# The order of split products inside each group: attention and the first MLP part

## The chip, the cores and the metric

One core of a Trainium2 chip. The metric is the device time of one execution in microseconds (us); lower is better. The engines are TensorE (PE, with its weight loads shown apart as PEld), VectorE (DVE), ScalarE (ACT), GpSimd (POOL) and SyncE (SP, which issues DMAs). Each takes its instructions in a fixed order and waits on semaphores for what others make.

## The reference

Linear attention with a feature map, then two MLP blocks, over 8 batches, 8 heads, 576 tokens, head width 64, model width 512. What matters here:

```python
def phi(x):
    proj = np.einsum('bhsd,df->bhsf', x, w_phi)
    proj = proj - np.max(np.abs(proj), axis=-1, keepdims=True)
    return np.concatenate([np.exp(proj), np.exp(-proj)], axis=-1)
q_p, k_p = (phi(q), phi(k))
kv = np.einsum('bhsf,bhsd->bhfd', k_p, v)      # key-value products, with z = sum of k_p beside them
num = np.einsum('bhsf,bhfd->bhsd', q_p, kv)    # numerators, with the denominators beside them
...
xn = (x - mu) / np.sqrt(var + 1e-06) * g_ln    # first MLP block
ch = np.maximum(xn @ w_ch1, 0.0) @ w_ch2
x = x + ch
...                                            # second block: cos and sin of x @ w_theta, token mixing, a channel MLP
```

All inputs are float32, and the kernel reaches that accuracy with the faster 32-bit matmul type by splitting: a value is the sum of a high part, rounded to that type, and a low part, the rest. A product of two split values is three matmuls into one PSUM accumulator: high by high, high by low, low by high.

## The kernel before, in words

**Attention.** 16 units (`Unit`), one for each of 4 pairs of batches and 4 pairs of heads, each with 9 token tiles of 128 in five groups (`GROUPS`: two tiles, two, one, two, two). The single tile of group 2 holds the last 64 tokens of one batch and the first 64 of the next, so it gives two slots of half zeros; in all there are ten slots. `keys` (line 310) makes the features of a group: `phi` (projection into PSUM tile `pj`, maximum `m`, difference `ys` on VectorE), two exponentials on ScalarE, the high part `kph` on ScalarE, then the low part `kpl` on VectorE (line 64; on GpSimd for two groups of the first five units). `values` (line 325) multiplies them with the split values `vh`, `vl` into the accumulator `kv`: for each slot and each of the two heads one call of `mm3`, that is three matmuls of 256 columns. The values are the stationary operand, and the features move. The key features are the factor made last.

`queries` makes the features of the queries, transposed, split into `qp` (high part by ScalarE, low part by GpSimd), and `numer` (line 404) multiplies them with the transposed key-value sums `kvh`, `kvl`: four accumulators `nm` in groups 2 and 4, each of two `mm3` calls of 288 columns. Units 0 to 4 do the numerators unsplit, unit 0 also the key-value products, each in one float32 matmul; these are not touched.

**First MLP part.** `Mlp` holds the first 4 of 16 hidden blocks of 128 (`NFA`), applied in attention's shadow to 18 chunks of 256 tokens. `mlp_a` normalises and transposes a chunk, splits it into `xh` (ScalarE) and `xl` (VectorE); `up` (line 189) makes two hidden blocks into a PSUM tile `ph`, each over 4 blocks of the model width, one `mm3` of 256 columns for each; `relu` splits the result into `hh` (ScalarE) and `hl` (VectorE); `down` (line 196) sums over the 4 hidden blocks into `ph` again, one `mm3` of 512 columns for each. After 650 us the rest of the kernel runs (the other 12 hidden blocks with fewer products by a matrix identity, then the second MLP block); the diff touches none of it.

**What sets the order.** The program is written as generators that are interleaved by `attention` and the loop behind it, but the order on each engine comes from a planner: it runs a model of all engines, and at each point gives an engine the instruction of highest rank (place in the program, moved by `high_priority`; the first MLP part is put back by 600 places, `MPRI`) whose inputs are there by that model. So matmuls of several accumulators come mixed on TensorE, but the matmuls of one accumulator stay in the program's order. On the chip each engine then follows the planned order, and an instruction that waits holds back all that is behind it. Accumulators are PSUM tiles: two for `pj`, one for `tr`, one for `kv`, two for `nm`, two for `ph`.

In the profile, `mm3` is lines 74 (high by high), 75 (stationary high by moving low) and 76 (stationary low by moving high). A trace row names the moving operand first: `kv<-kpl,vh` reads the low part of the key features.

Of the kernel before, what the change touches and what calls it, by code (L numbers as in the profile page):

```python
# [9 lines left out]
F32 = mybir.dt.float32  # L10
# [11 lines left out]
B, H, S, D = 8, 8, 576, 64  # L22
DM = 512
DFF = 2048
NF = 128
# [4 lines left out]
KC = DM // P  # L30
# [22 lines left out]
def body(ctx, tc, qT, kT, va, wbd, g, w1, w2, wth, wtok, wch, out):  # L53
    nc = tc.nc
    V, A, G, T, SY = nc.vector, nc.scalar, nc.gpsimd, nc.tensor, nc.sync
# [17 lines left out]
    def mm3(out_, lh, ll, rh, rl, start, stop, **kw):  # L73
        T.matmul(out_, lhsT=lh, rhs=rh, start=start, stop=False, **kw)  # L74
        T.matmul(out_, lhsT=lh, rhs=rl, start=False, stop=False, **kw)  # L75
        return T.matmul(out_, lhsT=ll, rhs=rh, start=False, stop=stop, **kw).ins  # L76
# [88 lines left out]
    class Mlp:  # L165
# [23 lines left out]
        def up(self, f, ph, xh, xl):  # L189
            h, l = self.w1[f // 2]  # L190
            for j in range(2):
                fs = slice((2 * (f % 2) + j) * P, (2 * (f % 2) + j + 1) * P)
                for c in range(KC):
                    mm3(ph[:, j, :], h[:, c, fs], l[:, c, fs], xh[:, c, :], xl[:, c, :], c == 0, c == KC - 1)

        def down(self, i, acc, hid):
            o = slice(i * P, (i + 1) * P)
            for f, (hh, hl) in enumerate(hid):
                for j in range(2):
                    wh, wl = self.w2[2 * f + j]  # L200
                    mm3(acc, hh[:, j, o], hl[:, j, o], wh, wl, f == 0 and j == 0, f == self.nf // 2 - 1 and j == 1)

        def relu(self, pool, ph):
            hh = pool.tile([P, 2, NC_], F32R, name="hh", bufs=2)
# [13 lines left out]
    ps_pj, ps_tr, ps_kv, ps_nm, ps_ph = pool("pj", 2), pool("tr", 1), pool("kv", 1), pool("nm", 2), pool("ph", 2)  # L218
# [26 lines left out]
    GROUPS = [[0, 1], [2, 3], [4], [5, 6], [7, 8]]  # L245
# [4 lines left out]
    class Unit:  # L250
# [74 lines left out]
        def values(self, gi, kh, kl):  # L325
            if gi == 0:
                self.acc = ps_kv.tile([D + 1, 2, 2 * NF], F32, name="kv")
            for i, t in enumerate(GROUPS[gi]):
                for sl in [t] if t < 4 else ([4, 5] if t == 4 else [t + 1]):
                    if sl == 5:  # L330
                        self.kv_done()
                        self.acc = ps_kv.tile([D + 1, 2, 2 * NF], F32, name="kv")
                    vh, vl = self.v[sl // 5]
                    for h in range(2):
                        j = 2 * i + h
                        rh = kh[:, j].rearrange("p s f -> p (s f)")
                        if kl is None:
                            T.matmul(self.acc[:, h, :], lhsT=vh[:, sl % 5, h, :], rhs=rh,
                                     start=sl in (0, 5) and h == 0, stop=sl in (4, 9), skip_group_check=True)
                            continue  # L340
                        rl = kl[:, j].rearrange("p s f -> p (s f)")
                        mm3(self.acc[:, h, :], vh[:, sl % 5, h, :], vl[:, sl % 5, h, :], rh, rl,
                            sl in (0, 5) and h == 0, sl in (4, 9), skip_group_check=True)
            if gi == 4:
                self.kv_done()

# [57 lines left out]
        def numer(self, gi):  # L404
            if gi in (2, 4):
                b = 0 if gi == 2 else 1
                kh, kl = self.kv[b]
                for h in range(2):
                    for hf in range(2):
                        nm = ps_nm.tile([D + 1, 288], F32, name="nm")  # L410
                        cs = slice(hf * 288, (hf + 1) * 288)
                        for s in range(2):
                            if kl is None:
                                T.matmul(nm, lhsT=kh[:, 2 * h + s, :], rhs=self.qp[b][0][:, h, s, cs], start=s == 0,
                                         stop=s == 1)
                                continue
                            mm3(nm, kh[:, 2 * h + s, :], kl[:, 2 * h + s, :], self.qp[b][0][:, h, s, cs],
                                self.qp[b][1][:, h, s, cs], s == 0, s == 1)
                        o = b * S + hf * 288
                        A.activation(self.num[:, h, o:o + 288], nm, AF.Copy)  # L420
                for t0 in [0] if b == 0 else [3, 6]:
                    self.norm(t0)
# [280 lines left out]
    def in_slot(n, slot, shape, dtype=F32R):  # L703
        return slot_pool(slot).tile([P, *shape], dtype, name="xs", tag=f"{n}{slot}")
# [15 lines left out]
    total, done, n = sum(w for _, w in work), 0, 0  # L720
    left = 6 * (NCH - 1 - chunk)
    for _ in gm:
        n += 1
        with tc.issue_after(ma.low), tc.issue_after(ma.high), tc.high_priority(offset=LOWP):
            while work and done < total * n / (left * SPREAD):
                g, w = work.pop(0)
# [466 lines left out]
    for r in range(2):  # L1193
        done = 0
        for ch in range(NQ):
            last = ch == NQ - 1
            if r and ch == LATE:
                t = in_slot("wa", 2, [7, DM])
                wths = [t[:, 2 * i:2 * i + 2] for i in range(3)]
                spare = f32(t[:, 6])  # L1200
                t = in_slot("wd", 2, [2, 2, DM])
                wths += [t[:, i] for i in range(2)]
            xs = cur
            acc = [ps_ac.tile([P, DM], F32, name=f"acc{i}") for i in range(2 * CT)]
# [50 lines left out]
    t = p_xb.tile([P, 4, 2, 2 * P], F32R, name="xs", tag="xt")  # L1255
# [198 lines left out]
```

## Time and profile before

| | |
|---|---|
| Time, median of 3 runs | 1651.89 us (1651.49 to 1654.31) |
| The profiled execution's own time | 1651.22 us |
| Its span, first to last instruction | 1649.4 us |
| TensorE busy (matmuls) | 1611.8 us, 98% |
| Weight loads busy | 1482.6 us, 90% |
| VectorE busy | 1270.1 us, 77% |
| ScalarE busy | 877.8 us, 53% |
| GpSimd busy | 715.4 us, 43% |
| Mean granted TensorE clock | 0.997 |

The shares are means over stages that differ. GpSimd, for one, does most of its work before 500 us. Matmuls are pipelined: the profile shows each with its full length, and the next starts before it ends, so the distance from start to start tells the rate. The number in brackets at the end of a row of the timeline is the time for which the engine stood idle before that instruction, and whose work ended it.

### The profile page before, as it was taken

To read this page: it belongs to the slowest core of one execution; us is meant where nothing else is said; L and a number is where in the kernel's file an instruction comes from. 1 tells how busy PE (TensorE), PEld (TensorE's weight loads), DVE (VectorE), ACT (ScalarE), POOL (GpSimd) and SP (SyncE) were. 2 spreads that over 40 slices of the span, in tenths; PEclk is the share of its full clock that TensorE was granted. 3 is DMA by queue.
4 is the path that set the end of the run, shared out by engine and by line. 5 is a ranking of instruction groups with operands and counts; after the bars stand their busy time and mean duration, and the time that the engine had idled before them with its cause. 6 is when DMAs were issued, how large, how long until landed. Compare 5 with 4: busy or idle time off the path is not lost.

```text
span 1649.4 us, 29031 instructions
## 1 busy us (share of the span) xinstructions
PE 1611.8 (98%) x11080; PEld 1482.6 (90%) x11080; DVE 1270.1 (77%) x2274; ACT 877.8 (53%) x1718; POOL 715.4 (43%) x561
## 2 busy tenths in 40 slices
PE   8899999999999999999999999999999999999998
PEld 6788999999999888899998989999889999999998
DVE  7989878888987774788777676778567878788784
ACT  6777767677776553445544434444444444544441
POOL 7876989899991001221111222211232443344430
PEclk9999999999999999999999999999999999999999
DMA  5334333333332644445547444463258565765754
GB/s 188 102 101 127 108 89 111 111 103 117 98 98 95 231 139 154 154 175 203 178 167 296 157 148 154 155 216 128 84 190 309 190 229 209 272 233 203 243 195 180
DMA packets 120329, 273.81 MB, mean 166 GB/s; under 512 B 9088, under 2 KB 62720, under 8 KB 112768
## 3 DMA queue, kind: packets, MB, share of 16 engines
q1 hardware_dynamic: 111984, 262.08, 46.6%
q10 hardware_dynamic: 8208, 9.90, 1.9%
q8 instruction: 87, 1.43, 0.3%
q14 instruction: 50, 0.41, 0.1%
HBM read 195.92 MB, written 73.92 MB: 164 GB/s over the span
## 4 chain that ended last, share of the span: by engine, by line
PE 85%; DVE 8%; DMA 3%; ACT 2%; issue 2%; POOL 1%; SPq 0%; DVEq 0%; ACTq 0%; POOLq 0%
PE acc L75 6%; PE acc L74 6%; PE acc L76 6%; PE pa L74 3%; PE ph L75 3%; PE ph L76 3%; PE pa L75 3%; PE pa L76 3%; PE ph L74 3%; PE mc L76 2%; PE mc L75 2%; PE mc L74 2%; PE ma L74 2%; PE ma L76 2%; PE ma L75 2%; PE pj L74 2%
## 5 line engine op out<-in xcount | busy, mean ns | idle before, releaser
L687 POOL TENSOR_TENSOR c<-xt 128x512 f32<-128x512 f32 x17 | 22.2, 1307 | 401.9 <-DMA xt<-xnd 324.4
L75 PE MATMUL acc<-wd,hb 128*128 128x512 f32 x432 | 170.1, 394 | 0.0
L74 PE MATMUL acc<-wd,hb 128*128 128x512 f32 x432 | 169.9, 394 | 0.0
L67 POOL TENSOR_TENSOR qp<-pf,qp 128x512 fp32r<-128x512 f32 (+1 forms) x120 | 147.8, 1255 | 13.3 <-ACT qp L61 12.7
L76 PE MATMUL acc<-wd,hb 128*128 128x512 f32 x432 | 152.9, 393 | 0.0
L304 DVE TENSOR_REDUCE m<-pj 128x4 f32<-128x512 f32 (+1 forms) x160 | 99.4, 625 | 39.8 <-PE pj L76 39.3
L64 DVE TENSOR_TENSOR a<-zf,a 128x1024 fp32r<-128x1024 f32 (+1 forms) x56 | 95.9, 1714 | 16.6 <-ACT a L61 16.5
L64 DVE TENSOR_TENSOR kpl<-pf,kph 128x1024 fp32r<-128x1024 f32 (+1 forms) x67 | 99.9, 1491 | 11.2 <-ACT kph L61 11.1
L61 ACT ACTIVATE a<-zf 128x1024 fp32r<-128x1024 f32 (+1 forms) x56 | 56.3, 1028 | 87.0 <-DVE xT L1014 31.2
L306 DVE TENSOR_TENSOR ys<-pj,m 128x512 f32<-128x512 f32 (+1 forms) x160 | 99.6, 628 | 2.1 <-ACT qf L391 0.5
L316 ACT ACTIVATE pf<-ys 128x512 f32<-128x512 f32 (+1 forms) x160 | 85.2, 584 | 26.7 <-DVE ys L306 20.3
L75 PE MATMUL kv<-kpl,vh 128*65 128x256 f32 x300 | 86.3, 288 | 6.7 <-DVE kpl L64 6.6
L75 PEld LDWEIGHTS acc<-wd,hb 128*128 128x128 f32 x432 | 81.7, 189 | 11.0
L74 PEld LDWEIGHTS acc<-wd,hb 128*128 128x128 f32 x432 | 81.7, 189 | 10.7
L76 PEld LDWEIGHTS acc<-wd,hb 128*128 128x128 f32 x432 | 78.3, 189 | 12.5
L74 PE MATMUL kv<-kph,vh 128*65 128x256 f32 x300 | 86.7, 289 | 0.0
L807 ACT ACTIVATE u<-pa 128x256 f32<-128x256 f32 x108 | 41.0, 380 | 84.9 <-PE pa L76 84.1
L76 PE MATMUL kv<-kph,vl 128*65 128x256 f32 x300 | 84.6, 282 | 0.0
L420 ACT ACTIVATE num<-nm 65x288 f32<-65x288 f32 x128 | 50.6, 401 | 50.1 <-PE nm L76 41.7
L74 PE MATMUL ma<-t,a 128*128 128x288 f32 x248 | 73.8, 298 | 1.1 <-DMA t<-wtkdt 0.9
L1126 POOL TENSOR_SCALAR k<-k 128x512 f32<-128x512 f32 x31 | 28.1, 907 | 106.1 <-ACT k L1125 106.1
L75 PE MATMUL ma<-t,a 128*128 128x288 f32 x248 | 73.5, 297 | 0.0
(413 smaller groups left out, 6283.5 us busy)
## 6 DMA issues: line engine op xcount, KB each, us to landing
t<-wtkdt SPq DMA_DIRECT2D x16, 1440.0 KB, 7.3
t<-wtkd SPq DMA_DIRECT2D x15, 1440.0 KB, 6.1
t<-wtkdt SPq DMA_DIRECT2D x16, 1152.0 KB, 6.8
xt<-xnd SPq DMA_DIRECT2D x34, 512.0 KB, 4.7
raw<-in_w SPq DMA_DIRECT2D x32, 512.0 KB, 4.7
in<-in_va SPq DMA_DIRECT2D x30, 325.0 KB, 3.1
xd<-xo SPq DMA_DIRECT2D x48, 192.0 KB, 2.7
x<-xd SPq DMA_DIRECT2D x36, 256.0 KB, 2.9
```

Of the source, the lines that this page charges most:

```text
L61: A.activation(dst, src, AF.Copy)
L64: return V.tensor_tensor(dst, src, f32(hi), op=ALU.subtract).ins
L67: G.tensor_tensor(dst, src, f32(hi), op=ALU.subtract)
L74: T.matmul(out_, lhsT=lh, rhs=rh, start=start, stop=False, **kw)
L75: T.matmul(out_, lhsT=lh, rhs=rl, start=False, stop=False, **kw)
L76: return T.matmul(out_, lhsT=ll, rhs=rh, start=False, stop=stop, **kw).ins
L304: V.tensor_reduce(m[:, :2 * n], pv, axis=AX.X, op=ALU.max, apply_absolute_value=True)
L306: marks.append(V.tensor_tensor(ys[:, :2 * n, :], pv, m[:, :2 * n].unsqueeze(2).to_broadcast([P, 2 * n, NF]), op=ALU.subtract).ins)
L316: A.activation(kp[:, :2 * n, s, :], ys[:, :2 * n, :], AF.Exp, scale=sc)
L420: A.activation(self.num[:, h, o:o + 288], nm, AF.Copy)
L807: A.activation(t, ps, AF.Copy)
L1126: G.tensor_scalar(k, k, -MAGIC, 1.0, op0=ALU.add, op1=ALU.mult)
```

## The change

In each group of split products the order changes. Those that read the high part of the factor made last (the key features in `values`, the query features in `numer`, the tokens in `up`, the hidden values in `down`) come first, with both parts of the other factor; those that read its low part come last. In `values` a group is all slots of a group of tiles (for the single tile, which crosses to the next accumulator, each slot is its own group); in `numer` it is one accumulator `nm`; in `up` one hidden block; in `down` two hidden blocks of one `relu`. The number of matmuls, their shapes and operands are the same.

```diff
         def up(self, f, ph, xh, xl):
...
                 for c in range(KC):
-                    mm3(ph[:, j, :], h[:, c, fs], l[:, c, fs], xh[:, c, :], xl[:, c, :], c == 0, c == KC - 1)
+                    for w in (h, l):
+                        T.matmul(ph[:, j, :], lhsT=w[:, c, fs], rhs=xh[:, c, :], start=c == 0 and w is h, stop=False)
+                for c in range(KC):
+                    T.matmul(ph[:, j, :], lhsT=h[:, c, fs], rhs=xl[:, c, :], start=False, stop=c == KC - 1)
 
         def down(self, i, acc, hid):
             o = slice(i * P, (i + 1) * P)
+            last = self.nf // 2 - 1
             for f, (hh, hl) in enumerate(hid):
                 for j in range(2):
-                    wh, wl = self.w2[2 * f + j]
-                    mm3(acc, hh[:, j, o], hl[:, j, o], wh, wl, f == 0 and j == 0, f == self.nf // 2 - 1 and j == 1)
+                    for w in self.w2[2 * f + j]:
+                        T.matmul(acc, lhsT=hh[:, j, o], rhs=w, start=f == 0 and j == 0 and w is self.w2[0][0],
+                                 stop=False)
+                for j in range(2):
+                    T.matmul(acc, lhsT=hl[:, j, o], rhs=self.w2[2 * f + j][0], start=False, stop=f == last and j == 1)
...
         def values(self, gi, kh, kl):
...
+            slots = [(i, sl) for i, t in enumerate(GROUPS[gi])
+                     for sl in ([t] if t < 4 else [4, 5] if t == 4 else [t + 1])]
+            for run in [[s] for s in slots] if gi == 2 else [slots]:
+                if run[0][1] == 5:
+                    self.kv_done()
+                    self.acc = ps_kv.tile([D + 1, 2, 2 * NF], F32, name="kv")
+                for k, parts in ((kh, (0, 1)), (kl, (0,))):
+                    for i, sl in run if k is not None else []:
+                        for h in range(2):
+                            for n in parts:
+                                v = self.v[sl // 5][n]
+                                if v is not None:
+                                    T.matmul(self.acc[:, h, :], lhsT=v[:, sl % 5, h, :],
+                                             rhs=k[:, 2 * i + h].rearrange("p s f -> p (s f)"),
+                                             start=sl in (0, 5) and h == 0 and n == 0 and k is kh,
+                                             stop=sl in (4, 9) and (k is kl or kl is None), skip_group_check=True)
...
-                            mm3(nm, kh[:, 2 * h + s, :], kl[:, 2 * h + s, :], self.qp[b][0][:, h, s, cs],
-                                self.qp[b][1][:, h, s, cs], s == 0, s == 1)
+                            for w in (kh, kl):
+                                T.matmul(nm, lhsT=w[:, 2 * h + s, :], rhs=self.qp[b][0][:, h, s, cs],
+                                         start=s == 0 and w is kh, stop=False)
+                        for s in range(2) if kl is not None else ():
+                            T.matmul(nm, lhsT=kh[:, 2 * h + s, :], rhs=self.qp[b][1][:, h, s, cs], start=False,
+                                     stop=s == 1)
```

## Rows read from the trace of the kernel before

**Rows 1.** The page: engine, busy us, share of the span, instructions.
```profile
PE 1611.8 (98%) x11080; PEld 1482.6 (90%) x11080; DVE 1270.1 (77%) x2274; ACT 877.8 (53%) x1718; POOL 715.4 (43%) x561
```
**Rows 2.** Busy time by stretch: length, then PE, PEld, DVE, ACT, POOL, PEclk, DMA.
```profile
0.00:560.00 560.00, 534.15 (x4089) 491.66 (x4090) 473.18 (x931) 394.09 (x753) 430.54 (x353) 0.99 0.39 118
```
**Rows 3.** Waits of TensorE up to 560 us: us in total, times, longest.
```profile
PE kv L75 <- DVE kpl L64: 6.6, 7, 2.3
PE pj L74 <- DVE ys L306: 4.7, 8, 1.6
...
PE pj L74 <- DVE rd L437: 2.6, 3, 1.0
PE tr L381 <- DVE ys L306: 1.4, 2, 0.8
```
**Rows 4.** Matmuls by line and shape: count, busy us, mean ns, idle before.
```profile
L75 PE MATMUL kv<-kpl,vh 128*65 128x256 f32 x300 | 86.3, 288 | 6.7 <-DVE kpl L64 6.6
...
L75 PE MATMUL ph<-xl,w 128*128 128x256 f32 x224 | 64.2, 287 | 0.4 <-DVE xl L64 0.4
...
L75 PE MATMUL nm<-qp,kvh 128*65 128x288 f32 x176 | 51.8, 295 | 0.0
```
**Rows 5.** Timeline at 380 us: start, duration, instruction, idle before it.
```profile
379.77 0.28 PE L74 MATMUL ph<-xh,w 128*128 128x256 f32 x1
...
381.34 0.28 PE L76 MATMUL kv<-kph,vl 128*65 128x256 f32 x1
...
382.05 0.28 PE L76 MATMUL kv<-kph,vl 128*65 128x256 f32 x1
```
**Rows 6.** Timeline at 205 us, ahead of the longest wait.
```profile
204.38 0.31 PE L74 MATMUL kv<-kph,vh 128*65 128x256 f32 x1
...
205.31 0.36 PE L74 MATMUL ph<-xh,w 128*128 128x256 f32 x1 [0.62 <-DVE xl L64]
...
206.81 2.54 DVE L64 TENSOR_TENSOR kpl<-pf,kph 128x1024 fp32r<-128x1024 f32 x1
```
**Rows 7.** Timeline: the eight waits of TensorE for a low part.
```profile
41.89 0.34 PE L75 MATMUL kv<-kpl,vh 128*65 128x256 f32 x1 [0.72 <-DVE kpl L64]
...
59.28 0.34 PE L75 MATMUL kv<-kpl,vh 128*65 128x256 f32 x1 [0.94 <-DVE kpl L64]
...
209.40 0.48 PE L75 MATMUL kv<-kpl,vh 128*65 128x256 f32 x1 [2.33 <-DVE kpl L64]
...
280.52 0.33 PE L75 MATMUL kv<-kpl,vh 128*65 128x256 f32 x1 [0.30 <-DVE kpl L64]
...
297.55 0.33 PE L75 MATMUL kv<-kpl,vh 128*65 128x256 f32 x1 [0.53 <-DVE kpl L64]
...
302.03 0.39 PE L75 MATMUL ph<-xl,w 128*128 128x256 f32 x1 [0.37 <-DVE xl L64]
...
381.17 0.33 PE L75 MATMUL kv<-kpl,vh 128*65 128x256 f32 x1 [1.12 <-DVE kpl L64]
...
421.84 0.33 PE L75 MATMUL kv<-kpl,vh 128*65 128x256 f32 x1 [0.67 <-DVE kpl L64]
```
**Rows 8.** Waits of TensorE from 560 to 650 us.
```profile
PE ph L74 <- ACT hh L206: 1.3, 3, 0.7
```
**Rows 9.** Busy time by stretch around the longest wait; 0.50 is PEclk.
```profile
207.00:209.40 2.40, 0.07 (x2) 0.00 (x1) 2.40 (x2) 1.51 (x2) 2.40 (x2) 0.50 0.10 15
209.40:213.50 4.10, 4.10 (x19) 4.10 (x20) 4.10 (x8) 0.00 (x0) 4.10 (x6) 0.50 0.20 59
```
**Rows 10.** Timeline at 43 us, after the first of the eight waits.
```profile
43.25 0.36 PE L74 MATMUL pj<-wb,kh 128*128 128x256 f32 x1 [0.56 <-DVE ys L306]
```
**Rows 11.** Waits of VectorE up to 560 us.
```profile
DVE m L304 <- PE pj L76: 39.3, 33, 4.1
```

More of the change, by code (lines that the diff above doesn't have):

```diff
@@ L327, in values @@
                 self.acc = ps_kv.tile([D + 1, 2, 2 * NF], F32, name="kv")
[L328 to L343, printed above, removed]
+            slots = [(i, sl) for i, t in enumerate(GROUPS[gi])
[14 more added lines that the diff above has]
+                                             stop=sl in (4, 9) and (k is kl or kl is None), skip_group_check=True)
             if gi == 4:
```

## The prediction

> **What bounds the kernel now.** I read the page's busy shares first, then the waits of TensorE in the stretch that the diff touches, then the order of time around each of those waits. TensorE is busy for 98% of the span, with a weight load beside every one of its 11080 matmuls [rows 1], so what is taken off TensorE's queue, or out of its idle time, is mostly taken off the end. But the busy share hides the place that matters. Up to 560 us, where attention and most of the first MLP part run, TensorE is busy 534 of 560 us, while VectorE is busy 473 and GpSimd 431 [rows 2]: three engines close to full, in queues of fixed order, so each runs late against another now and then. The waits of TensorE there are the budget of this change. The largest sum is for `kpl`, the low part of the key features that VectorE makes: 6.6 us in 7 waits. Beside it stand waits for `ys` (4.7 and 1.4 us) and for `rd` (2.6), which no split product can shorten [rows 3].
>
> **What the diff moves.** No instruction is added or removed. Each triple (high by high, high by low, low by high) stays, 300 triples in the key-value products, 288 in `up` (224, and 64 more in another bank), 176 in the numerators (by [rows 4]), 144 in `down`; only their order inside a group changes. DMAs, VectorE, ScalarE and GpSimd keep their instructions; their order can shift, because the planner orders all engines against its own clock. So there are three terms: what each visible wait loses, what the clock gives back, and what is late next.
>
> **Term 1, the waits for a low part.** The pattern is the same at all eight places: one `kv` product of line 74 runs, then whatever else the planner had ready, then line 75 waits for `kpl`, and behind it in the queue stand the other products of the group. Of those, the ones that need only `kph` were runnable throughout. A group of two tiles has 4 slot-heads, so 12 products, of which 8 need only the high part: 7 more than the one that went ahead. The single-slot groups have 6 products, 4 of them high: 3 more. One 256-column product takes 0.118 us in a stream at the full clock (six of them from 381.34 to 382.05, [rows 5]). So the cover is 0.83 us in a long group and 0.35 us in a short one. In `up` the same holds: line 74 had gone ahead alone at 205.31 and 379.77 [rows 5, 6], and seven more high products of its first half now stand with it, another 0.83 us.
>
> Against the eight waits [rows 7]: 0.72 at 41.89 (a short group) loses 0.35; 0.94 at 59.28 loses 0.83; 2.33 at 209.40 has both covers and loses 1.65; 0.30 at 280.52 and 0.53 at 297.55 go; 1.12 at 381.17 has both covers and goes; 0.67 at 421.84 goes; the one for `xl` at 302.03, 0.37, goes. Sum: 0.35 + 0.83 + 1.65 + 0.30 + 0.53 + 1.12 + 0.67 + 0.37 = 5.8 us. Whether the high products fill the wait itself or an earlier hole is the same to the end: at 205.31 the `ph` product waited 0.62 us too [rows 6], and the seven `kv` products would run there; either way they no longer stand behind 209.40.
>
> The other groups give nothing directly. `down` waits for the high part `hh` (1.3 us, 3 times, [rows 8]), which is as early in the new order as in the old. The numerators' low parts come from GpSimd; no wait of theirs stands in the list of waits, so moving them back covers nothing. Bounds of this term: 0, if the planner uses the new freedom to put the low products exactly where it believes `kpl` lands (below, the rival of no change), and 7.0, all eight waits. I take 5.8, the sum by cover, since each wait above has its high products provably queued behind it.
>
> **Term 2, the clock.** During the wait before 209.40 the granted clock is 0.50, the lower of its two levels (1.2 of 2.4 GHz), and it stays there until 213.5, in which 4.10 us hold 19 matmuls, 0.216 us each, against 0.118 at full rate [rows 9]. So the longest wait costs a second time: 19 x 0.098 = 1.9 us. The page on TensorE of the Trainium skill ("TensorE: Matmul & The Clock Gate", section "What's actually happening") has the rule that the throttled state is the default and activity releases it; the trace agrees, with 0.50 after the wait. If the high products land inside the wait this 1.9 us goes; if they run ahead, at 204.4 to 206.3, the hole in front of `kpl` is as long as it was and the clock falls all the same. What stood ahead of it, a product at 204.38 and one at 205.31, says that they run ahead, so I take 0 and keep 1.9 for the range.
>
> **What is late next.** The wait of 0.56 us for `ys` at 43.25 [rows 10] comes 1.4 us after the first of the eight; its VectorE work (`kpl`, then `ys`) is not moved, so it swallows that place's 0.35. After the others the next wait for VectorE is further off (after 209.40 TensorE has work queued for many microseconds), and VectorE, which waits on `pj` 33 times for 39.3 us in this stretch [rows 11], moves earlier with TensorE. I give back 0.35 and no more.
>
> **A rule that speaks against the change.** In the old order the first two products of a triple share their stationary operand; in `up`, the key-value products and the numerators (288 + 300 + 176 = 764 triples) the new order parts them. The trace has 11080 loads for 11080 matmuls, so no load is shared now [rows 1]. The Trainium skill ("TensorE: Matmul & The Clock Gate", section "Step-by-step: what each phase is for") says that weights usually stay put over many matmuls, so that one load serves several. By that rule parting them would cost a load each; a load is 1482.6 / 11080 = 0.134 us, so 764 x 0.134 = 102 us if nothing hid it. By the row it costs nothing, and I take 0.
>
> **Sum.** 5.8 - 0.35 = 5.45 us off the profiled execution's own 1651.22 us, which makes 1645.8. The profiled execution lies 0.67 us under the median of the three runs (1651.89), so in their terms 1646.4.
>
> **Rivals.**
>
> *Nothing (the planner hands the cover back).* Low products keep the group's rank, so the planner issues them as soon as its own model says that `kpl` is there, and other work behind them. VectorE's lateness against that model (one `kpl` took 2.54 us at 206.81, [rows 6]) is then waited for as before. For: in the old order too other products were run between line 74 and line 75. Against: these holes had only a few products to offer, one or two at 204 and 379, so there was room. Time: between 1651.9 and about 1649, with a few tenths per wait saved.
>
> *Slower: the runs of high products hold back what feeds VectorE.* Seven products put in one block ahead of `pj` and the transposes delay these by up to 0.83 us, and VectorE waits on `pj` 33 times already [rows 11]. TensorE then meets VectorE late at `ys` and `rd`: 8 + 3 + 2 = 13 waits there now [rows 3]. If each grows by 0.83, that is 10.8 us; against 5.45 saved it ends 5.3 us up, at 1657.2; with the saving lost as well it would be 1662.7. It decides from 5.45 / 0.83, about 7 of the 13. For: VectorE is busy 473 of 560 us, so it has little to catch up with. Against: the work of the block had to be done anyway, and in the old order the same products held `pj` back just as long, only after the wait.
>
> *More than forecast.* The freer order also closes holes of the other kinds, and the clock's 1.9 us comes back: all of term 1 (7.0), 1.9, and half of the 8.7 us at `ys` and `rd` make 13.3, which gives 1638.6.
>
> *The shared load* (the rule above): 1651.9 + 102 = 1754. The equal counts leave it less than 1 in 100.
>
> **Chances.** Forecast (1641 to 1649) 0.48; more than forecast (below 1641) 0.08; nothing (1649 to 1655) 0.23; slower by its mechanism (above 1655) 0.21. What a measurement can tell from no change is 0.2%, or 3.3 us, so between 1648.6 and 1655.2 counts as the same. Within the forecast case nearly all lies under 1648.6; that makes faster 0.55, same 0.24, slower 0.21. The range from 1638.5 to 1657 leaves out about one in ten on either side: it takes in the best case above and the slower rival with the saving kept. The forecast's own range is 1641 to 1649.
>
> **What would show it.** Right: TensorE's waits for `kpl` in the first 560 us fall from 6.6 to under 2 us, `kv` products come in runs of eight by `kph` and then four by `kpl`, the waits on `ys` and `rd` stay near 8.7 in sum, and the first MLP part ends 4 to 6 us earlier, while everything after it has the same length. Wrong: waits of the same length on line `kpl` after the run of eight (no change); or waits on `ys` and `rd` above 14 us, with VectorE idle longer for `pj` (slower); or a difference that arises after 650 us, where no touched line runs. A granted clock of 1.00 from 200 to 300 us, with the wait before the low products still there, would show that I was wrong about term 2.

## The result, and the profile after

The changed kernel takes 1678.54 us, median of 6 runs (1674.3 to 1680.55), against 1653.09 for the kernel before in its 6 runs: a ratio of 1.015, interval 1.0138 to 1.0161. It is 25 us slower; the forecast was 1646.4, and the range ended at 1657. The profiled execution took 1674.3 us, the least of the six, with a mean granted TensorE clock of 0.996 where the kernel before had 0.997; the other five, 1676.8 to 1680.6 us, had 0.991 to 0.994. So the profile shows 4 us less of the loss than the median, and the lower clock is a part of the median's loss: 0.003 to 0.006 of some 1678 us is 5 to 10 us at most, an estimate from these clocks.

The page of the changed kernel, engine, busy us, share of the span and instructions:

```profile
PE 1617.4 (97%) x11080; PEld 1484.7 (89%) x11080; DVE 1286.1 (77%) x2274; ACT 877.9 (52%) x1718; POOL 714.7 (43%) x561
```

The counts are those of [rows 1]. But VectorE needs 16.0 us more for the same 2274 instructions (1286.1 against 1270.1): something changed on an engine that the diff does not touch. Where the 23.1 us of span arose is read from the first matmul of the next part, `acc`, in the tile's view of the kernel before and then of the one after (durations min/median/max in ns, then first and last start in us):

```profile
L74 PE MATMUL acc<-wd,hb x432: 387/395/501, 649.5 to 1238.8; 128*128 128x512 f32 x144
```
```profile
L74 PE MATMUL acc<-wd,hb x432: 387/395/497, 670.1 to 1261.2; 128*128 128x512 f32 x144
```

So 20.6 of the 23.1 us are lost before that point, in the part that the diff touches. Busy time up to that point, in the kernel before and then in the one after (columns as in [rows 2]):

```profile
0.00:649.50 649.50, 622.33 (x4666) 571.01 (x4666) 526.86 (x1020) 437.35 (x831) 435.62 (x357) 0.99 0.39 121
```
```profile
0.00:670.10 670.10, 626.08 (x4667) 571.51 (x4667) 541.16 (x1021) 437.27 (x831) 432.23 (x357) 0.99 0.38 117
```

TensorE has done the same work there. It stood idle for 44.0 us where it had been 27.2, which is 16.8 of the 20.6 us; in the other 3.8 it was busy, longer for as many matmuls. Up to 560 us in the changed kernel:

```profile
0.00:560.00 560.00, 521.44 (x3979) 476.56 (x3980) 469.61 (x878) 380.18 (x728) 427.91 (x353) 0.99 0.35 107
```

By 560 us TensorE has issued 3979 matmuls, 110 fewer than in [rows 2], and has stood idle for 38.6 us where it had been 25.9. Which waits grew is in the list of TensorE's waits up to 560 us, after the change:

```profile
PE kv L347 <- DVE kpl L64: 6.8, 8, 1.9
PE pj L74 <- DVE ys L313: 6.1, 8, 1.6
PE tr L388 <- DVE ys L313: 4.8, 3, 3.2
...
PE ph L541 <- DVE xn L537: 3.5, 3, 1.8
PE nm L362 <- ACT kvs L356: 2.9, 3, 1.7
PE ph L197 <- DVE xl L64: 1.4, 1, 1.4
PE pj L74 <- DVE rd L448: 1.4, 1, 1.4
```

Two rows of the kernel before, in the same list, stand for the short ones there:

```profile
PE ph L530 <- DVE xn L526: 0.7, 1, 0.7
...
PE nm L355 <- ACT kvs L349: 0.7, 1, 0.7
```

Against [rows 3] the wait that the change was to shorten, for `kpl`, is as long as it was (6.8 after 6.6), and others have grown: for `ys` from 4.7 + 1.4 to 6.1 + 4.8, and for `xn` and `kvs` from 0.7 each to 3.5 and 2.9. They are spread over many places. VectorE in turn waits longer for TensorE; this row answers to [rows 11], 39.3 there:

```profile
DVE m L311 <- PE pj L76: 48.6, 33, 4.3
```

One place shows how the cover went. This is the timeline of the changed kernel at 250 us, first TensorE, then VectorE:

```profile
249.67 0.33 PE L347 MATMUL kv<-kph,vh 128*65 128x256 f32 x1
...
250.53 0.28 PE L347 MATMUL kv<-kph,vl 128*65 128x256 f32 x1
...
252.29 0.47 PE L428 MATMUL nm<-qp,kvh 128*65 128x288 f32 x2
254.62 0.57 PE L347 MATMUL kv<-kpl,vh 128*65 128x256 f32 x3 [1.86 <-DVE kpl L64]
```
```profile
249.91 1.17 DVE L537 TENSOR_SCALAR xn<-x,lmv,lrs 128x512 f32<-128x512 f32 x1
250.99 0.68 DVE L313 TENSOR_TENSOR ys<-pj,m 128x512 f32<-128x512 f32 x1
251.59 0.67 DVE L311 TENSOR_REDUCE m<-pj 128x4 f32<-128x512 f32 x1
252.19 2.38 DVE L64 TENSOR_TENSOR kpl<-pf,kph 128x1024 fp32r<-128x1024 f32 x1
```

The run of eight high products stands where it was promised, its starts from 249.67 to 250.53, and 3.8 us lie between the end of its last product and the end of the wait. Yet `kpl` comes too late: `kph` was ready (the first high product reads it at 249.67), but VectorE's queue has `xn`, `ys` and `m` of other chains first, and `kpl` itself takes 2.38 us. Over the 75 key groups, worked out from the traces, the first low product stands 4.58 us behind the end of its `kph`, on average, where it had stood 3.86: 0.72 us of room. Over those after 140 us (54 before, 55 after; room there 0.70 us), VectorE starts `kpl` 1.32 us after `kph`, where it had been 0.74: 0.58 us of the room are gone before VectorE begins.

### The profile page after: what moved, and what is told of

The parts are those of the page before. It is cut to its first block, busy times and chain, and to the rows that moved or that the text cites. A ratio compares the mean times of both kernels' runs of the same rounds, so it can differ in the third digit from the quotient of the medians.

```text
span 1672.5 us, 29000 instructions
## 1 busy us (share of the span) xinstructions
PE 1617.4 (97%) x11080; PEld 1484.7 (89%) x11080; DVE 1286.1 (77%) x2274; ACT 877.9 (52%) x1718; POOL 714.7 (43%) x561
## 4 chain that ended last, share of the span: by engine, by line
PE 76%; DVE 7%; DMA 3%; ACT 2%; issue 2%; POOL 0%; SPq 0%; ACTq 0%; DVEq 0%; POOLq 0%
PE acc L75 5%; PE acc L74 5%; PE acc L76 5%; PE ph L205 4%; PE kv L347 3%; PE pa L74 3%; PE pa L75 3%; PE pa L76 3%; PE ph L195 3%; PE nm L425 2%; PE mc L76 2%; PE mc L74 2%; PE mc L75 2%; PE ma L76 2%; PE ma L74 2%; PE ma L75 2%
## 5 line engine op out<-in xcount | busy, mean ns | idle before, releaser
L67 POOL TENSOR_TENSOR qp<-pf,qp 128x512 fp32r<-128x512 f32 (+1 forms) x120 | 140.9, 1198 | 8.4 <-ACT qp L61 8.1
L311 DVE TENSOR_REDUCE m<-pj 128x4 f32<-128x512 f32 (+1 forms) x160 | 99.6, 625 | 49.2 <-PE pj L76 48.6
L64 DVE TENSOR_TENSOR kpl<-pf,kph 128x1024 fp32r<-128x1024 f32 (+1 forms) x67 | 107.4, 1602 | 7.0 <-ACT kph L61 5.4
L205 PE MATMUL ph<-w,hh 128*128 128x512 f32 x288 | 78.9, 393 | 1.4 <-ACT hh L213 1.4
L347 PE MATMUL kv<-kph,vh 128*65 128x256 f32 x300 | 78.9, 292 | 0.0
L74 PE MATMUL ma<-t,a 128*128 128x288 f32 x248 | 73.8, 298 | 2.3 <-DMA t<-wtkdt 2.2
L347 PE MATMUL kv<-kph,vl 128*65 128x256 f32 x300 | 76.0, 283 | 0.0
L75 PE MATMUL ma<-t,a 128*128 128x288 f32 x248 | 73.5, 297 | 0.0
L76 PE MATMUL ma<-t,a 128*128 128x288 f32 x248 | 73.1, 297 | 0.0
```

What stands on the lines that cost most here:

```text
L64: return V.tensor_tensor(dst, src, f32(hi), op=ALU.subtract).ins
L67: G.tensor_tensor(dst, src, f32(hi), op=ALU.subtract)
L205: T.matmul(acc, lhsT=hh[:, j, o], rhs=w, start=f == 0 and j == 0 and w is self.w2[0][0], stop=False)
L311: V.tensor_reduce(m[:, :2 * n], pv, axis=AX.X, op=ALU.max, apply_absolute_value=True)
L347: T.matmul(self.acc[:, h, :], lhsT=v[:, sl % 5, h, :], rhs=k[:, 2 * i + h].rearrange("p s f -> p (s f)"), start=sl in (0, 5) and h == 0 an ...
```

## The experiments

All times are medians, each ratio against runs of the kernel before on the same chip. Four questions were asked, in this order: which group's change loses; whether it is the products' order or the layout that the planner makes of it; what a new layout costs when nothing is won or lost by it; and which engine or edge carries the loss.

### One group at a time

Each kernel is the one before with one hunk of the diff. The first, as a diff:

```diff
-            for i, t in enumerate(GROUPS[gi]):          # values: triples
...
+                for k, parts in ((kh, (0, 1)), (kl, (0,))):   # values: high first; up, numer, down as before
```

> Only the key-value products in the new order (runs of 8 high, 4 low); up, numerators and down as before. Theory H (hold-back: the block of eight high products goes ahead of pj and of the transposes, VectorE gets its inputs late): this part alone carries most of the +25 us, 1667 to 1680, with VectorE's wait for pj above 45 us (39.3 before). Theory R (any new order makes the planner lay out all engines anew, and the plan's luck decides): anywhere from 1645 to 1670, and the four parts alone do not add up to +25. Theory U (the reorder of up does the harm): within 3 us of before, 1650 to 1656.

1661.78 us, ratio 1.0061 (1.0046 to 1.0076).

> Only up in the new order (per hidden block 8 products with the high part of the tokens, then 4 with the low part). H: within 4 us of before, 1649 to 1657, since these products have a low rank and only fill holes. U: 1665 to 1680. R: 1645 to 1670, unrelated to block size.

1664.79 us, 1.0073 (1.0056 to 1.0089).

> Only the numerators in the new order (4 high, then 2 low, per accumulator). H: 0 to +5 us, 1653 to 1658, a block of four is half as long as one of eight and comes twice per unit. U: within 3 us of before. R: 1645 to 1670.

1657.38 us, 1.0034 (1.0023 to 1.0046).

> Only down in the new order (4 products by the high part of the hidden values, then 2 by the low part, 512 columns each). H and U: within 3 us of before, 1650 to 1656: nothing waits for the low part there and nothing new can go ahead. R: 1645 to 1670 even here, since the order changes for the planner as well.

1663.96 us, 1.0072 (1.0054 to 1.0090).

All four lose: 9.5, 12.5, 5.1 and 11.7 us against 1652.27, 38.8 in sum where all together lose 25. All lie in the range of theory R, which is a wide one. Theory H misses three, theory U all four (`up` by 0.2 us only). VectorE's wait for `pj`, which H had above 45 us for `values` alone, was 39.2 there, and for `up` alone 33.4, less than the 39.3 of the kernel before:

```profile
DVE m L304 <- PE pj L76: 39.2, 27, 5.6
```
```profile
DVE m L307 <- PE pj L76: 33.4, 30, 2.9
```

`down` is the telling one. `down` was seen to wait for the high part `hh` alone [rows 8], which its hunk leaves in front, and no wait of TensorE for the low part `hl` was in the lists; still it costs 11.7 us. What its kernel has in common with the others is a new layout on every engine: about 250 of VectorE's 2275 places differ from the order before, and about 600 for `values`, though neither hunk has a VectorE instruction.

### The products' order and the layout taken apart

The planner can be made to keep an order: here each engine's order is taken from its plan for one kernel and laid as order-only edges on the other one's instructions, place by place in the program.

```diff
+        for seq in order or ():                     # the planned order of each engine that is held
+            for a, b in zip(seq, seq[1:]):
+                tc.add_manual_dep(traced[b], traced[a].name, info, reason="order")
```

With all five engines held as in the kernel before, only the order inside the groups is new (some 1530 of TensorE's 10980 places).

> The changed products, with the order of every engine held as the planner made it for the kernel before (edges that fix issue order alone): each matmul stands at its old place in TensorE's queue, only inside a group the high products take the first of the group's places and the low ones the last. Theory R (the change is good, the new plan of all engines is what costs): 1644 to 1651, as the cover sum of the prediction says (5.8 us at most), TensorE's waits for kpl down from 6.6 to about 1. Theory I (the new inner order itself is worse on the chip): 1665 or more. Theory H (the block of high products held ahead of pj and the transposes) expects no loss either, since nothing is pulled forward here.

1649.91 us in 10 runs, ratio 0.9986 (0.9976 to 0.9996): a little faster than before (by 0.04 to 0.24%; its runs spread from 1645.5 to 1653.7), and the fastest median of this study. Its waits of TensorE up to 560 us (in the kernels with held orders the lines are others: 1666 is `values`, 1383 makes `kpl`, 1707 the transposes):

```profile
PE pj L1393 <- DVE ys L1632: 4.9, 7, 1.6
...
PE pj L1393 <- DVE rd L1767: 3.2, 3, 1.5
PE tr L1707 <- DVE ys L1632: 2.3, 3, 0.9
PE kv L1666 <- DVE kpl L1383: 1.9, 5, 0.7
```

The wait for `kpl` falls from 6.6 to 1.9 us, and the idle time of TensorE up to 560 us from 25.9 to 23.4:

```profile
0.00:560.00 560.00, 536.60 (x4092) 493.03 (x4093) 476.37 (x932) 393.66 (x754) 430.92 (x353) 0.99 0.39 118
```

The place of the longest one, 209.40 in [rows 7], in this kernel's timeline:

```profile
206.81 0.35 PE L1514 MATMUL ph<-xh,w 128*128 128x256 f32 x1 [0.57 <-DVE xl L1383]
207.86 0.43 PE L1393 MATMUL pj<-wb,kh 128*128 128x256 f32 x1 [0.70 <-DVE ys L1632]
...
208.52 0.41 PE L1666 MATMUL kv<-kph,vl 128*65 128x256 f32 x1
...
209.80 0.41 PE L1666 MATMUL kv<-kph,vl 128*65 128x256 f32 x1
210.92 0.48 PE L1666 MATMUL kv<-kpl,vh 128*65 128x256 f32 x1 [0.70 <-DVE kpl L1383]
```

Seven high products fill the hole and 0.70 us are left of 2.33. So the inner order does what it says, and with the same products and the same inner order the time is 1649.9 us in one layout and 1678.5 in the other. What the change loses, it loses by the layout. The other corner is the triples in the changed kernel's layout, all orders held:

> The missing corner: the products of the kernel before (triples), in the changed kernel's layout, with the orders of all five engines held; only the order inside each group is the old one. If the loss lies in the layout and the inner order is slightly good in either (2 to 6 us): 1679 to 1686, with TensorE's waits for kpl above the changed kernel's 6.8 us. If the new inner order is itself what loses: 1655 to 1668.

1730.84 us, 1.0463 (1.0428 to 1.0497), far outside both expectations. Its two longest kinds of wait up to 560 us:

```profile
PE kv L75 <- DVE kpl L64: 40.2, 22, 5.4
PE kv L75 <- POOL kpl L67: 9.5, 12, 1.8
```

With the old order inside the groups the new layout waits 49.7 us for `kpl`; with the new order 6.8. The new layout lives on the cover: it lets `kpl` come late because the high products stand in front. Part of the 52 us is the clock: the mean granted clock is 0.979 here and 0.996 in the changed kernel's profile, and 0.017 of 1731 us is 29 us at most, an estimate. This corner was badly chosen for its second purpose (a layout made for one order is bound to be bad for the other), but it shows that in either layout high products first are better, by 2 us in the old and 52 in the new, and that the layout costs 1678.5 − 1649.9 = 28.6 us with the new products in both (27.6 when each is taken against the kernel before in its own series of runs).

TensorE planned anew, the other four engines held as before:

> The changed products; VectorE, ScalarE, GpSimd and SyncE held in the order of the plan before, TensorE planned anew, so that high products run ahead of other work wherever the planner likes. H: slow, 1665 to 1680, since the blocks of eight stand ahead of pj and the transposes as in the changed kernel. R in the narrow form (the loss comes from the new order of VectorE, ScalarE and GpSimd): 1645 to 1655.

1658.72 us, 1.0037 (1.0024 to 1.0051), between the two expectations. VectorE waits longer for `pj` here:

```profile
DVE m L1630 <- PE pj L1395: 50.3, 36, 5.5
```

And the reverse, the old products with the four other engines held in the changed kernel's order and TensorE planned anew:

> The products of the kernel before, in triples; VectorE, ScalarE, GpSimd and SyncE held in the order that the planner made for the changed kernel, TensorE planned anew under that. R in the narrow form: as slow as the changed kernel or slower, 1672 to 1690, though no high product runs early. H: near the kernel before, 1650 to 1660.

1691.35 us, 1.0241 (1.0224 to 1.0258). So with the four engines in the new order it is slow with the old products too, by 39 us, even when TensorE is laid out to suit them; with those four in the old order the new products lose only 6.7. The 39 us have the weakness of the corner before: those four orders were made for products that give `kpl` time.

### What a new layout costs by itself

A first control changed one figure of the planner's model (its rate for matmuls, 10 to 10.2), meant to give a new layout of the same kernel.

> A control without the change: the kernel before, with the pace at which pieces of the first MLP part are handed out raised from 10 to 10.2, which moves a few pieces by one step and makes the planner lay out about as many places anew as down alone did (438 of 2274 on VectorE). R: slower by 3 to 15 us like the four parts, 1655 to 1667, since the plan before is a favourable one among its neighbours. H: within 3 us of before.

1652.76 us, 1.0004 (0.9995 to 1.0014). It failed as a control: matched by what the instructions are, only 62 of VectorE's 2275 places differ; the number in the expectation was counted by place in the program, which overstates it. Two exchanges that leave the amount of work and its dependences as they are did give new layouts (569 and 582 places): the order of the two loops around `numer`'s accumulators, and of the two pieces of the query tile that crosses batches. Each was run without and with the change.

```diff
-                for h in range(2):
-                    for hf in range(2):
+                for hf in range(2):
+                    for h in range(2):
```
```diff
-                parts = [(0, 512, 0, 64), (1, 0, 64, 64)]
+                parts = [(1, 0, 64, 64), (0, 512, 0, 64)]
```

> Control without the change: the kernel before, with the two loops over the four accumulators of numer exchanged (halves outside, heads inside). No product waits for more or less than it did, but the planner lays out all engines anew (569 of VectorE's 2275 places do not match the plan before; 558 for the changed kernel). Theory R (the plan before is a favourable one, and any new plan costs): slower by 5 to 25 us, 1657 to 1677. Theory H (the blocks of high products and what they push back are the cause): within 4 us of before, 1648 to 1656.

1654.84 us, 1.0019 (1.0007 to 1.0031), in the range of H and below that of R.

> The changed kernel with the same exchange of the two loops of numer: another plan of the same products. R: the loss of 25 us is a draw and not a property of the change, so this lies anywhere from 1650 to 1680, most likely lower than the changed kernel, near 1663, the middle of the four parts alone. H: 1670 to 1685, as the blocks of high products are the same.

1656.72 us, 1.0030 (1.0015 to 1.0044). This is in the range of R and far below that of H. With the loops exchanged the change loses 1.9 us and not 25, and the two intervals overlap, so even these 1.9 are not clear of the noise. Its `kpl` wait is short too, and 4076 matmuls are done by 560 us, 97 more than in the changed kernel:

```profile
PE kv L347 <- DVE kpl L64: 1.9, 3, 1.2
```

> Second control without the change: the two pieces of the split query tile in exchanged order (582 of VectorE's places do not match). R: 1657 to 1677. H: 1648 to 1656.

1657.54 us, 1.0035 (1.0018 to 1.0051), at the lower end of R's range; single runs spread from 1652.6 to 1665.1.

> The changed kernel with the exchanged pieces of the split query tile. R: 1650 to 1680, again most likely near 1663. H: 1670 to 1685.

1674.58 us, 1.0136 (1.0121 to 1.0151): 17.0 us more than the same exchange alone, and in both ranges.

So a neutral exchange costs 2.2 and 4.9 us against the 1652.67 of these runs, and the change on top of it 1.9 and 17.0. The loss depends on the layout that is drawn; whether the change makes a bad draw likelier, two pairs can't show.

### Which engine, which edge

VectorE's order held as before, all other engines planned anew; then ScalarE, GpSimd and SyncE held, VectorE and TensorE planned anew:

> The changed kernel's products, with VectorE's order alone held as the kernel before has it; TensorE, ScalarE, GpSimd and SyncE are laid out by the planner anew. With all five orders held it was 1649.9 us, with all but TensorE's 1658.7, with none 1678.5. If VectorE's new order is what carries the loss (kpl queued behind m and ys of other groups): 1657 to 1662, with TensorE's waits for kpl in the first 560 us under 4 us. If the loss is a draw of the whole layout, which no single engine carries: 1664 to 1680.

1660.84 us, 1.0043 (1.0024 to 1.0063): the time is as VectorE's queue would have it, but the wait for `kpl`, expected under 4 us, is not:

```profile
PE kv L1666 <- DVE kpl L1383: 5.6, 6, 2.5
```

> Control to the run with VectorE's order alone held (1660.8 us): the changed products with the orders of ScalarE, GpSimd and SyncE held as before, VectorE and TensorE laid out anew (407 of VectorE's 2275 places don't match those of before). If VectorE's order is the lever: 1670 to 1680. If holding any engine brings the layout near the old one, and with it the time: 1657 to 1664.

1651.89 us, 1.0004 (0.9992 to 1.0016), under both ranges, with VectorE's wait for `pj` as before:

```profile
DVE m L1630 <- PE pj L1395: 39.9, 31, 3.9
```

The control takes that reading away. With VectorE and TensorE free and the three others held nothing at all is lost; the run with VectorE held was no proof that its queue is the cause. A hold may do no more than keep the layout near the old one, but then holding four engines, which lost 6.7 us, should have kept it nearer than holding three. The orders of ScalarE, GpSimd and SyncE as the carriers of the loss are the other reading, and none of them was held or freed by itself. Two edges were then tried alone, by a high rank for one instruction in the changed kernel: `kpl` on VectorE, and `pj` on TensorE (this one in the kernel before as well).

```diff
+            with tc.high_priority(offset=HIP):
-            (lo_cut if self.idle and gi in KPOOL else lo_vec)(kl[:, :2 * n], kp[:, :2 * n], kh[:, :2 * n])
+                (lo_cut if self.idle and gi in KPOOL else lo_vec)(kl[:, :2 * n], kp[:, :2 * n], kh[:, :2 * n])
```
```diff
+                with tc.high_priority(offset=HIP):
-                mm3(ps[:, i, :], xh[:, c], xl[:, c], wb[:, 0, :], wb[:, 1, :], True, True)
+                    mm3(ps[:, i, :], xh[:, c], xl[:, c], wb[:, 0, :], wb[:, 1, :], True, True)
```

> The changed kernel, with the making of kpl (the low part of the key features) put at high rank on VectorE; nothing else is edited. If kpl queued behind other groups' ys and m on VectorE carries the loss: 1658 to 1665, with the mean time from the end of kph to the start of kpl back from 1.32 to about 0.8 us. If the loss is a draw of the layout: anything from 1655 to 1685, and the delay of kpl doesn't go with the time. If kpl ahead of ys only moves the wait: TensorE's waits for kpl fall by 4 us or more, those for ys grow by as much, and the time stays within 5 us of 1678.

1674.74 us, 1.0138 (1.0122 to 1.0154). The delay of `kpl` behind `kph` fell only from 1.32 to 1.16 us and TensorE's wait for it from 6.8 to 5.2; `tr` now waits 5.7 us for `ys`:

```profile
PE tr L389 <- DVE ys L313: 5.7, 4, 3.2
PE kv L348 <- DVE kpl L64: 5.2, 5, 1.9
```

That is 3.8 us of the 25. Only the time fits the third line of the expectation: the wait for `kpl` fell by 1.6 us and not by 4, and those for `ys`, 10.9 us in sum before this edit, are 10.6 with the 4.9 at `pj`. A rank that cut the delay only by 0.16 us leaves the first line untried.

> The changed kernel, with the pj products (from which VectorE takes its maxima m) put at high rank on TensorE. By the rival of the prediction (blocks of high products hold back pj, VectorE waits for it and then runs late): VectorE's wait of m for pj, 48.6 us, falls to 39 or less, and the time is 1655 to 1662. If pj comes late for another reason, or VectorE's own order is at fault: the time stays above 1668. If a draw: anywhere, and not along with the wait for pj.

1668.46 us, 1.0097 (1.0078 to 1.0117), short of the gain that the rival asked for. VectorE's wait for `pj` collapses, and TensorE's for `ys` grows instead; up to 560 us, this kernel's row for `m` and for `pj`:

```profile
DVE m L312 <- PE pj L76: 16.0, 21, 2.6
```
```profile
PE pj L74 <- DVE ys L314: 10.2, 13, 2.1
```

> Control: the kernel before, with the same high rank for its pj products. If early pj is worth something by itself, it gains here as well: 1645 to 1650, with VectorE's wait for pj well under 39.3 us. If it only undoes what the change does, nothing: 1651 to 1656. If each new layout costs: 1655 to 1660.

1664.34 us, 1.0076 (1.0060 to 1.0092), above all three ranges, with 24.2 us of that wait left. So 48.6 us of waiting for `pj` became 16.0 and bought 10 us in one kernel, and 39.3 became 24.2 and cost 12 in the other: the wait for `pj` is a companion of the loss and not its handle. Between these two the change costs 4.1 us.

## Why the prediction was wrong

**Term 1, the cover, came out nearly whole in the old layout.** It said that 5.8 us of the eight waits go and under 2 us stay at `kpl`; with the orders held 1.9 are left [rows 3, 7] and the wait for `xl` at line 75 is gone, so 5.1 of the 5.8 us went. At the longest wait the size is luck: it lost 2.33 − 0.70 = 1.63 us where the working said 1.65, but the working added the cover of `up` to that of `kv`, both at the full pace. In the trace above seven `kv` products fill the hole at 0.21 us each, and none of `up` is among them.

**Term 2, taken as 0, was right at its place, but not its reason.** The clock was taken to fall all the same around 209 us. With the orders held, the products from 208.52 on start 0.21 us apart and not 0.118, the pace of [rows 9], where the granted clock is 0.50, so 1.2 of 2.4 GHz. It is preceded by the waits at 206.81 and 207.86, which the change does not touch. But the longest wait was not shown to be what costs the clock. In the kernel before, the granted clock was at 0.50 before that wait began at 207.07, and in the changed kernel a longer one left it at 1.00; the row of the kernel before, then those of the changed one:

```profile
206.70:207.07 0.37, 0.37 (x3) 0.05 (x1) 0.37 (x3) 0.37 (x2) 0.37 (x2) 0.50 0.13 42
```
```profile
313.09 0.66 PE L388 MATMUL tr<-ident,ys 128*128 128x128 f32 x4 [3.16 <-DVE ys L313]
```
```profile
313.50:316.00 2.50, 2.50 (x23) 2.50 (x22) 2.50 (x5) 2.16 (x5) 1.78 (x2) 1.00 0.35 127
```

So it is not shown that the 1.9 us hang on that wait, as the working had it.

**"What is late next" was too small.** It gave back 0.35 us. With the orders held the waits for `rd` and for `ys` at `tr` grew by 0.6 and 0.9, those for `num` and `kvs` by 0.8 each: 3.1 us. Some other waits are shorter, and in all the idle time up to 560 us falls by 2.5 us; the medians differ by 2.2 (1649.9 against 1652.1). By these rows several of TensorE's feeders were near late, and a wait that goes uncovers the next.

**The step that failed** is a sentence ahead of the terms: VectorE, ScalarE and GpSimd "keep their instructions; their order can shift, because the planner orders all engines against its own clock". It was read as a remark, with no price and no bounds. It is the largest term: 28.6 us by the pair of held and free layout. The bounds of term 1, 0 to 7.0 us, left the same thing out; the end at 0 assumed that a planner which uses its freedom can at worst give the cover back. The cover was given back, nearly (the wait for `kpl` went from 6.6 to 6.8, and the room of 0.72 us per group lost 0.58 to VectorE's queue), so the rival of no change had its mechanism right for that wait; but at the same time the waits of other kinds grew by some 12 us up to 560 us, at `ys`, `xn` and `kvs` above all.

**The slower rival** had the right signs: VectorE waits longer for `pj` (48.6 after 39.3), and `ys` and `rd` stand at 6.1 + 4.8 + 1.4 us, 13.7 with two short rows for `rd` (0.8 and 0.6), near the 14 us named. Its mechanism is that blocks of high products hold back `pj`. The run with all orders held does not test it, since nothing is pulled forward there. TensorE's new order alone costs 6.7 us (1658.7 against 1652.1) of the 25, with that wait at 50.3, so the mechanism may carry a part. But the wait does not go with the loss: `values` alone loses 9.5 us with 39.2 and `up` alone 12.5 with 33.4, while TensorE and VectorE planned anew together lose nothing with 39.9. Nor is 0.83 us at each of 13 waits its size. The shared load, given less than 1 in 100, was out of the question as judged: with the orders held the triples are parted and nothing is lost.

**What stays open** is why this layout loses 25 us and the one with the loops exchanged 4. The four pairs with free layout lose 25.4, 1.9, 17.0 and 4.1 us, and the four hunks alone lose as well. But the first pair and the hunks start from the kernel before, which no edit of the layout without the change has beaten (0.7, 2.2, 4.9 and 12.2 us slower), and 1.9 is within the noise. That high products first tempt the planner into layouts that are worse on the chip is possible and not shown, and which of its beliefs about durations might mislead it was not tried. One candidate has numbers: in the new layout `kpl` takes 107.4 us in 67 instructions and before 99.9, so VectorE's work itself grows; why is open (below). It cannot be all: the changed kernel with the pieces exchanged has VectorE busy for 1278.0 us, 8 fewer, and loses nearly as much, and the kernel before with the loops exchanged has 1278.6 and loses 2.2.

## What to carry to other kernels

Where a planner lays out all engines, an edit of the order on one engine is two edits: what it does in the old layout, and a new layout for every engine; price the second from neutral exchanges, here 2 to 5 us of 1652, and from single hunks, here 5 to 12, before you trust a gain of 5. To keep the first without the second, hold the old orders by edges that order and add no wait of their own: that version, at 1649.9 us, is 0.14% faster than the kernel before (interval 0.04 to 0.24%) and 28.6 us faster than the changed one. And when one engine's order held brings a loss back, run the control with another engine's order held before you name the engine.

## What was not expected of the hardware

The same instruction on VectorE, `kpl` of 128x1024, took 2.38 us at 252.19 (above) and 1.21 at 313.55. At 252.19 GpSimd runs its own two-input subtractions through the whole time; at 313.55 it stands idle for the first half:

```profile
250.75 4.56 POOL L67 TENSOR_TENSOR qp<-pf,qp 128x512 fp32r<-128x512 f32 x4
```
```profile
313.55 1.21 DVE L64 TENSOR_TENSOR kpl<-pf,kph 128x1024 fp32r<-128x1024 f32 x1
```
```profile
314.13 1.11 POOL L58 TENSOR_SCALAR qh<-in 128x512 fp32r<-128x512 f32 x1 [2.75 <-DMA in<-in_qT]
```

Over the changed kernel's 52 of that shape, the 11 with under 30% of their time beside a two-input GpSimd instruction took 1.31 us on average, the 32 with over 90% took 1.83, and the 9 between took 1.89. The Trainium skill ("SBUF — State Buffer", section "Who interferes with whom") says that a VectorE instruction with two inputs in SBUF contends with a GpSimd instruction that reads SBUF; the averages agree. Single rows do not always: three of the 32 took 1.22 us or less, and the one at 52.32, with one-input GpSimd instructions beside it all the time, took 1.21. For the whole group the page of the profile has 107.4 us after and 99.9 before, at the same count:

```profile
L64 DVE TENSOR_TENSOR kpl<-pf,kph 128x1024 fp32r<-128x1024 f32 (+1 forms) x67 | 107.4, 1602 | 7.0 <-ACT kph L61 5.4
```

That the 7.5 us come from more overlap is not shown. In the kernel before, 10 of the 52 had under 30% and 31 over 90%, nearly as after, and those 31 took 1.67 us on average where the 32 took 1.83: instructions with as much beside them took longer, and no run here shows why. What the rows do show is that the same instruction takes between 1.2 and 2.4 us by its place in the layout, one more reason why a new layout is not free.
